# Output products of an attention layer, from columns on the partitions to tokens on the partitions

## The chip, the cores and the metric

The kernel runs on one core of a Trainium2 chip. The metric is the device time of one execution in microseconds. Most executions of one kernel agree within 0.3%; the kernel before took 551.26 us in the median of the first three runs (551.1 to 551.76). The span that a trace gives, from the first to the last instruction, is about 1.8 us shorter than the time of the same run (552.08 and 550.3 us for the profiled run of the kernel before).

Engine names in the profile: PE is TensorE's matmuls and PEld its weight loads, DVE the vector engine, ACT the scalar engine, POOL the one that issues some of the DMAs, SP the one that issues most of them and has no computation in these traces. STT in the prediction is DVE's operation SCALAR_TENSOR_TENSOR.

## The reference, cut to what matters

Attention with 16 query heads of 256, 512 keys, 2048 tokens; its output is multiplied by wo, gated, and added to x.

```python
# x: 2048 x 448;  o: 2048 tokens x 4096 (16 heads x 256);  wo: 4096 x 448
p = softmax(scores)                    # per head
o = einsum("bhqk,bhkd->bhqd", p, v)    # "P V"
s = o.transpose(...).reshape(B, Sq, Hq * Dh) @ wo
g = silu(ffn(xn))                      # the gate
return x + s * g
```

The kernel works on 512 tokens at a time. After the 16 heads of such a chunk it multiplies o by wo in one block, which this text calls a **burst**. There are four; each of the first three stands between a P V and Q matmuls of the next chunk, and the last one ends the kernel.

A burst uses Winograd's form of Strassen's scheme: tokens, contraction and columns are each halved, and seven products of sums take the place of eight. The sums of o are made by DVE (tile `sr`), those of wo once beforehand (tile `wt`).

## The kernel before: the parts that matter

wo's part is the stationary operand and o moves, so a product comes out with columns of the result on partitions. Each half has N2 = 192 columns, which are 128 + 64, so they are cut into pieces of 64 that fill the array two at a time; 64 columns are left over and multiplied plainly.

```python
N2 = (D - R) // 2                         # 192;  D = 448, R = 64, HC = 256 tokens

def product(j, b, rhs, hs, first, reads):     # one of the seven
    for h in hs:                              # two 64-column pieces, side by side in the array
        pair(0, HC, wt[:, WAT[j], h, 0:R], rhs(h), wt[:, WAT[j], h, R:P], rhs(h), ...)
    for h in hs[::2]:                         # the third piece, of two heads
        pair(HC, QC, wt[:, WAT[j], h, M2], rhs(h), wt[:, WAT[j], h + 1, M2], rhs(h + 1), False)
...
def plain():                                  # the 64 columns left over: 64 matmuls a burst
...
def turned(k):                                # four DMA transposes a burst: columns -> tokens
    dma_t(sT[:, :, k, :], xs[k], ...)
```

The last burst takes 14 heads. Then come the last two P V, and the last two heads are multiplied by wo apart, into banks where the burst's result is turned by matmuls with the identity:

```python
burst(c)                                      # c = 3, 14 heads
pv(late.pop(0)); pv(late.pop(0))
for t4, b, c0, c1 in ends[:3]:
    turn(t4, b, c0, c1)                       # matmuls with ident
...
    wo_mm(t4, b, ...)                         # o of heads 14 and 15, times wo
    wo_fin(c, t4, b, c0, c1)                  # scale, gate, add x, send
```

The gate is made early, by `down`, 128 tokens at a time, and waits in DRAM. DVE writes a tile of it into a ring of four slots, and SP sends it:

```python
K.op("dve", ... out=g2w[:, t % 4, :] ...)
dma("sp", g2d[t], g2w[:, t % 4, :], (b_g2w[t % 4],), (b_g2d[t],))
```

A scheduler in the kernel puts a semaphore wait wherever an operation reads what another engine wrote, or writes what another still reads.

The softmax here doesn't subtract the row's maximum and nothing guards it: scores larger than these inputs give would overflow.

Of the kernel before, what the change touches and what calls it, by code (L numbers as in the profile page):

```python
# [6 lines left out]
ALU = mybir.AluOpType  # L7
# [161 lines left out]
def bass_recurrent_scan__sliding_block_cached__geglu_ffn__prompt_kernel(  # L169
# [31 lines left out]
    CUT = D - P  # L201
# [5 lines left out]
    N2 = (D - R) // 2  # L207
# [3 lines left out]
    with es:  # L211
# [57 lines left out]
        b_xr = [[K.buf(a + (i * D + lo) * 2, (hi - lo) * 2) for lo, hi in ((0, CUT), (CUT, D))] for i in range(NXR)]  # L269
        tmp, a, _ = place("tmp", [P, 2, QC], F32)  # L270
        b_tmp = [[K.buf(a + (i * QC + lo) * 4, (hi - lo) * 4) for lo, hi in ((0, CUT), (CUT, QC))] for i in range(2)]

        tmpb, _, _ = place("tmpb", [P, 2, 2 * QC], BF16, at=a)
# [3 lines left out]
        wt, a_wt, a_w3 = place("wt", [P, 7, Hq, N2], F16)  # L277
# [3 lines left out]
        w3, _, rw_end = place("w3", [P, NCO, R], F16)  # L281
        w3b, _, _ = place("w3b", [P, NCO, R], BF16, at=a_w3)
        b_w3 = [K.buf(a_w3 + i * NCO // NB * R * 2, NCO // NB * R * 2) for i in range(NB)]
        NL = 4
        wo, a, a2 = place("wo", [P, NL, D], BF16, at=rw + WAT[0] * Hq * N2 * 2)
        assert NL * D <= Hq * N2
        b_wo = K.buf(a, NL * D * 2)
# [40 lines left out]
        a_c = b_p32[-1].hi - 8 * HC * 4  # L328
        assert a_c + 4 * HC * 4 >= a_p + 4 * HB * HC * 2
        cc, _, _ = place("cc", [P, 4, 2, HC], F32, at=a_c)  # L330
        b_cc = [[K.buf(a_c + (i * 2 + j) * HC * 4, HC * 4) for j in range(2)] for i in range(4)]
        g2w, a_s, a2 = place("g2w", [P, 4, D], BF16, at=at)
        b_g2w = sbuf_bufs(a_s, D * 2, 4)
        b_gz = sbuf_bufs(a_s, D * 2, 2)
        b_xz = [K.buf(a_s + (2 * D + lo) * 2, (hi - lo) * 2) for lo, hi in ((0, CUT), (CUT, D))]
        sT, _, at = place("sT", [P, 4, 3, P], BF16, at=at)
        b_sT = [K.buf(a_s, 12 * P * 2) for k in range(3)]
        b_xs = [K.buf() for k in range(4)]
        sN, _, at = place("sN", [P, 2, P], BF16, at=at)
        b_sN = K.buf(at - 2 * P * 2, 2 * P * 2)  # L340
# [66 lines left out]
        act(tmp[:, 1, 0:1], epst[:, :], ACT.Sqrt, (b_epst,), (b_tmp[1][0],))  # L407
# [134 lines left out]
        def down(c, pairs):  # L542
            for t4 in range(4):
                t = c * 4 + t4
                b = bk(pairs, t4)
                mms([(bank[b][:, 0:D], actT[:, c % 2, f, t4 * P:(t4 + 1) * P], wd[:, f, :], f == 0, f == NF - 1)
                     for f in range(NF)], [b_wd] + b_actT[c % 2], (b_ps[b],))
                s = t % 2
                act(tmp[:, s, 0:D], bank[b][:, 0:D], ACT.Tanh, (b_ps[b],), b_tmp[s], scale=0.5)
                K.op("dve", lambda e, t=t, b=b, s=s: e.scalar_tensor_tensor(  # L550
                    out=g2w[:, t % 4, :], in0=tmp[:, s, 0:D], scalar=1.0, in1=bank[b][:, 0:D],
                    op0=ALU.add, op1=ALU.mult), b_tmp[s] + [b_ps[b]], (b_g2w[t % 4],))
                dma("sp", g2d[t], g2w[:, t % 4, :], (b_g2w[t % 4],), (b_g2d[t],))
# [47 lines left out]
        act(tmp[:, 1, 0:1], nhalf[:, :], ACT.Gelu_apprx_tanh, (b_nhalf,), (b_tmp[1][0],))  # L601
# [28 lines left out]
        M2 = slice(P, N2)  # L630
# [4 lines left out]
        def cast_wt(j, i):  # L635
            if j == 7:
                sl, o, x, b = slice(i * NCO // NB, (i + 1) * NCO // NB), w3, w3b, b_w3
            else:
                sl, o, x, b = slice(i * Hq // NB, (i + 1) * Hq // NB), wt[:, WAT[j]], wtb[:, WAT[j]], b_wt[j]
            act(o[:, sl, :], x[:, sl, :], ACT.Copy, b[i:i + 1], b[i:i + 1], scale=WS)  # L640
# [6 lines left out]
        CASTS = [(18, (j, i)) for j in (0, 4, 7) for i in range(NB)] + [(40, (j, i)) for j in (2, 1) for i in range(NB)]  # L647
# [10 lines left out]
        for n in range(4, NU, 2):  # L658
# [11 lines left out]
            if n == 14:  # L670
                load_wt(0, 0, 0)
                load_wt(4, 0, 1)
                dma("pool", w3b[:, :, :], A_wo.rearrange("(c p) d -> p c d", p=P)[:, :, D - R:D], (), b_w3)
# [10 lines left out]
            if n == 32:  # L684
# [6 lines left out]
                for t in range(NXR):  # L691
                    dma("pool", xr[:, t, :], x_view[:, t, :], (), b_xr[t])
# [46 lines left out]
        def pv(m):  # L739
            h = m % Hq  # L740
            g, x = h // 2, m % NPT
            for e in range(2):
# [5 lines left out]
                o, f = (oTh, WS) if m < NS - LAG else (oT, 1.0)  # L748
                if e == 0:
                    act(o[:, i, :], bank[b], ACT.Copy, (b_ps[b],), (b_oT[i],), scale=f)  # L750
                else:
                    K.op("dve", lambda v, i=i, b=b, o=o, f=f: v.tensor_scalar(  # L752
                        o[:, i, :], bank[b], f, None, op0=ALU.mult), (b_ps[b],), (b_oT[i],))

        def wo_mm(t4, b, c0=0, c1=D, lo=NCO - 4, hi=NCO):

            mms([(bank[b][:, c0:c1], oT[:, i, t4 * P:(t4 + 1) * P], wo[:, i - NCO + NL, c0:c1], False, i == NCO - 1)
                 for i in range(lo, hi)], b_oT[lo:hi] + [b_wo], (b_ps[b],))

        def turn(t4, b, c0=0, c1=D):  # L760

            tok = slice(t4 * P, (t4 + 1) * P)
            lst = [(0, 0, tok, slice(0, P)), (P, 2, tok, HALF[0]), (N2, 1, tok, slice(0, P)), (N2 + P, 2, tok, HALF[1]),
                   (2 * N2, 3, slice(t4 % 2 * P, t4 % 2 * P + P), HALF[t4 // 2])]
            lst = [x for x in lst if c0 <= x[0] < c1]
            mms([(bank[b][:, lo:lo + k.stop - k.start], xs[j][:, q], ident[:, k], i == 0, False)
                 for i, (lo, j, q, k) in enumerate(lst)], b_xs + [b_ident], (b_ps[b],))

        def wo_end(t, c0, c1, mult, bt, y):

            x, bx = (xr[:, t % NXR, :], b_xr[t % NXR]) if t < NT - 1 else (g2w[:, 2, :], b_xz)
            g, bg = (g2[:, t % NG2, :], b_g2[t % NG2]) if t < NT - 2 else (g2w[:, t % 2, :], b_gz[t % 2])
            bx = [bx[i] for i in range(2) if (c0 < CUT, c1 > CUT)[i]]
            mult(g, bg)
            if t + NG2 < NT - 2:
                load_g2(t + NG2)
            add("dve", x[:, c0:c1], y[:, c0:c1], x[:, c0:c1], bt + bx, bx)
            dma("sp" if t >= NT - 4 else "pool", out_view[:, t, c0:c1], x[:, c0:c1], bx, ())
            if t + NXR < NT - 1:
                dma("pool", xr[:, t % NXR, :], x_view[:, t + NXR, :], (), b_xr[t % NXR])  # L780
            if t == NT - 5:
                K.reuse(b_gz + b_xz)
                for i in range(2):
                    dma("pool", g2w[:, i, :], g2d[NT - 2 + i], (b_g2d[NT - 2 + i],), (b_gz[i],))
                dma("pool", g2w[:, 2, :], x_view[:, NT - 1, :], (), b_xz)
# [4 lines left out]
        def wo_fin(c, t4, b, c0=0, c1=D):  # L790
            t = c * 4 + t4
            s = t % 2
            bt = [b_tmp[s][i] for i in range(2) if (c0 < CUT, c1 > CUT)[i]]
            if t4:
                y = tmpb[:, s, 0:D] if c0 == 0 else tmpb[:, s, CUT:CUT + D]

            def mult(g, bg):
                if t4 == 0:
                    K.op("dve", lambda e: e.scalar_tensor_tensor(  # L799
                        out=tmp[:, s, c0:c1], in0=bank[b][:, c0:c1], scalar=0.5, in1=g[:, c0:c1],  # L800
                        op0=ALU.mult, op1=ALU.mult), (b_ps[b], bg), bt)
                    return
                act(y[:, c0:c1], bank[b][:, c0:c1], ACT.Copy, (b_ps[b],), bt, scale=0.5)
                add("dve", y[:, c0:c1], y[:, c0:c1], g[:, c0:c1], bt + [bg], bt, ALU.mult)
            wo_end(t, c0, c1, mult, bt, tmp[:, s, :] if t4 == 0 else y)

        o_view = oTh.rearrange("p (h e) (r q) -> p e r h q", e=2, r=2)
        HALF = (slice(0, R), slice(R, P))
        xs = [xnT[:, k, 0:QC] for k in range(4)]

        def product(j, b, rhs, hs, first, reads):

            lst = []

            def pair(lo, hi, l0, r0, l1, r1, st):
                for u, l, r in ((0, l0, r0), (1, l1, r1)):
                    lst.append((bank[b][HALF[u], lo:hi], l, r, st, False))
            for h in hs:
                pair(0, HC, wt[:, WAT[j], h, 0:R], rhs(h), wt[:, WAT[j], h, R:P], rhs(h), first and h == hs[0])
            for h in hs[::2]:  # L820
                pair(HC, QC, wt[:, WAT[j], h, M2], rhs(h), wt[:, WAT[j], h + 1, M2], rhs(h + 1), False)
# [219 lines left out]
```

## Time and profile before

| | kernel before |
|---|---|
| time, median | 551.26 us |
| span in the trace | 550.3 us |
| PE busy | 98% of the span, 91% of the chain that ended last |
| first burst, start to the Q matmuls | 21.96 us |
| last burst, start to the end of the span | 32.05 us |

A burst is found in PE's timeline by its operands, `oTh,wt` and `sr,wt`. Matmuls are pipelined, so the cost of a group is read from the start of one to the start of the next, not from its busy time. The lines are in the prediction below.

### The profile page before, as it was taken

To read this page: it belongs to the slowest core of one execution; us is meant where nothing else is said; L and a number is where in the kernel's file an instruction comes from. 1 tells how busy PE (TensorE), PEld (TensorE's weight loads), DVE (VectorE), ACT (ScalarE), POOL (GpSimd) and SP (SyncE) were. 2 spreads that over 40 slices of the span, in tenths; PEclk is the share of its full clock that TensorE was granted. 3 is DMA by queue.
4 is the path that set the end of the run, shared out by engine and by line. 5 is a ranking of instruction groups with operands and counts; after the bars stand their busy time and mean duration, and the time that the engine had idled before them with its cause. 6 is when DMAs were issued, how large, how long until landed. Compare 5 with 4: busy or idle time off the path is not lost.

```text
span 550.3 us, 11945 instructions
## 1 busy us (share of the span) xinstructions
PE 540.5 (98%) x4649; PEld 294.7 (54%) x4674; DVE 360.0 (65%) x833; ACT 314.2 (57%) x795; POOL 41.4 (8%) x80
## 2 busy tenths in 40 slices
PE   8999999999999999999999999999999999999996
PEld 5554444445444444984444469544444974444594
DVE  6664735764457757945766786477568856767784
ACT  5433535763548858226866850498488037867603
POOL 1140500000000000003001000110100003002000
PEclk9999999999999999999999999999999999999999
DMA  9566289903325827313962850377267214855801
GB/s 286 125 184 151 61 280 307 162 1 84 92 48 115 154 58 153 65 31 76 169 139 59 151 123 7 57 155 154 74 112 158 45 31 113 155 116 135 149 33 35
DMA packets 177001, 63.29 MB, mean 115 GB/s; under 512 B 159808, under 2 KB 173648, under 8 KB 176944
## 3 DMA queue, kind: packets, MB, share of 16 engines
q1 hardware_dynamic: 172960, 52.76, 45.3%
q0 software_dynamic: 3216, 9.18, 5.8%
q8 instruction: 37, 0.61, 0.5%
q10 hardware_dynamic: 768, 0.57, 0.3%
q14 instruction: 20, 0.16, 0.1%
HBM read 20.22 MB, written 3.67 MB: 43 GB/s over the span
## 4 chain that ended last, share of the span: by engine, by line
PE 91%; DMA 2%; DVE 2%; ACT 2%; issue 1%; SPq 0%; ACTq 0%; DVEq 0%
PE bank L373 91%; ACT p L726 2%; DMA pT<-pn 2%; DVE pn L733 1%; DMA x<-in_A_x_dram 1%; DVE rden L730 0%; DVE tmpb L367 0%; SPq L358 0%; DVE qT L711 0%; DVE stats L420 0%; DVE tmp L799 0%; DVE sr L367 0%; DVE oTh L752 0%; ACT qT L364 0%; DVE g2w L367 0%
## 5 line engine op out<-in xcount | busy, mean ns | idle before, releaser
L726 ACT ACTIVATE p<-bank 128x512 f32<-128x512 f32 x256 | 150.5, 595 | 24.7 <-DVE pn L733 18.9
L373 PE MATMUL bank<-pT,va 128*128 128x512 bf16 x512 | 120.8, 379 | 0.3 <-DMA pT<-pn 0.3
L373 PE MATMUL bank<-kT,qT 128*128 128x512 bf16 x487 | 117.8, 379 | 2.3 <-ACT qT L364 1.0
L733 DVE TENSOR_SCALAR pn<-p,rden 128x512 bf16<-128x512 f32 x256 | 113.1, 484 | 9.6 <-DMA pT<-pn 5.5
L373 PE MATMUL bank<-xnT,wq 64*128 64x512 bf16 x768 | 94.9, 376 | 0.0
L373 PE MATMUL bank<-xnT,wgu 64*128 64x512 bf16 (+2 forms) x768 | 83.9, 350 | 0.5 <-ACT xnT L364 0.4
L373 PEld LDWEIGHTS bank<-pT,va 128*128 128x128 bf16 x512 | 49.6, 98 | 61.6 <-DMA pT<-pn 2.5
L373 PEld LDWEIGHTS bank<-kT,qT 128*128 128x128 bf16 x512 | 49.3, 98 | 62.0 <-issue 3.8
L364 ACT ACTIVATE qT<-bank 128x512 bf16<-128x512 f32 x76 | 44.1, 596 | 53.4 <-PE bank L373 51.8
L711 DVE CAST qT<-bank 128x512 bf16<-128x512 f32 x52 | 35.1, 692 | 44.0 <-PE bank L373 43.9
L373 PEld LDWEIGHTS bank<-xnT,wq 64*128 64x128 bf16 x768 | 36.7, 94 | 46.3 <-ACT p L726 2.1
L373 PEld LDWEIGHTS bank<-xnT,wgu 64*128 64x128 bf16 x768 | 37.1, 94 | 37.3 <-issue 0.7
L539 DVE TENSOR_TENSOR actT<-bank,gl 128x512 bf16<-128x512 f32 x56 | 37.8, 690 | 26.5 <-PE bank L373 19.9
L364 ACT ACTIVATE gl<-bank 128x512 bf16<-128x512 f32 x56 | 33.2, 597 | 37.1 <-PE bank L373 35.0
L730 DVE RECIPROCAL rden<-rsum 128x2 f32<-128x2 f32 x128 | 21.2, 166 | 48.5 <-ACT p L726 48.2
L726 ACT ACTIVATION_READ_ACCUMULATOR p<-bank 128x1 f32 x256 | 51.4, 201 | 0.0
L373 PE MATMUL bank<-wd,actT 128*128 128x448 bf16 x224 | 43.0, 353 | 0.0
L752 DVE TENSOR_SCALAR oTh<-bank 128x512 f16<-128x512 f32 x62 | 42.4, 684 | 0.0
L373 PE MATMUL bank<-sr,wt 128*64 128x256 f16 x744 | 41.5, 273 | 0.5 <-DVE sr L367 0.5
L364 ACT ACTIVATE xnT<-bank 128x256 bf16<-128x256 f32 (+2 forms) x12 | 4.9, 417 | 63.4 <-PE bank L373 62.8
L373 PEld LDWEIGHTS bank<-sr,wt 128*64 128x64 f16 x744 | 40.1, 110 | 1.4 <-DVE sr L367 0.7
L358 POOL DMA_DIRECT2D g<-g_all x14 | 7.5, 537 | 387.1 <-DVE tmpb L367 387.1
(71 smaller groups left out, 428.3 us busy)
## 6 DMA issues: line engine op xcount, KB each, us to landing
wtb<-in_A_wo_dram POOLq DMA_DIRECT2D x4, 768.0 KB, 7.2
wq<-in_A_wq_dram SPq DMA_DIRECT2D x2, 1536.0 KB, 9.2
va<-in_A_v_cache_dram SPq DMA_DIRECT2D x8, 256.0 KB, 6.4
pT<-pn SPq DMA_TRANSPOSE x128, 2.8
g_all<-g2w SPq DMA_DIRECT2D x16, 112.0 KB, 2.0
xr<-in_A_x_dram POOLq DMA_DIRECT2D x15, 112.0 KB, 2.3
wd<-in_B_w_down_dram SPq DMA_DIRECT2D x1, 1568.0 KB, 7.5
g<-g_all POOLq DMA_DIRECT2D x14, 112.0 KB, 2.3
```

The source lines that it names most:

```text
L358: K.op(q, lambda e, o=o, i=i: e.dma_start(o, i), reads, writes, dma=True)
L364: K.op("act", lambda e, o=o, i=i: e.activation(o, i, func, scale=scale), reads, writes)
L373: ins = e.matmul(o, lhsT=l, rhs=r, start=st, stop=sp, skip_group_check=True)
L539: K.op("dve", lambda e: e.tensor_tensor(actT[:, c % 2, f, :], bank[b + 1], gl[:, s, :], ALU.mult), (b_ps[b + 1], b_gl[s]), (b_actT[c % 2][ ...
L711: K.op("dve", lambda v, s=s, b=b: v.tensor_copy(qT[:, s, 1, :], bank[b + 1]), (b_ps[b + 1],), (b_qT[s][1],))
L726: K.op("act", lambda e, b=b, r=r, z=z: e.activation(p32[:, z, :], bank[b], ACT.Exp, scale=att_scale, accum_out=rsum[:, r:r + 1]), (b_ps[b] ...
L730: K.op("dve", lambda e, r=r: e.reciprocal(rden[:, r - 1:r + 1], rsum[:, r - 1:r + 1]), b_rsum[r - 1:r + 1], b_rden[r - 1:r + 1])
L733: K.op("dve", lambda e, r=r - 1 + t, z=(n - 1 + t) % NP32, y=y, t=t: e.tensor_scalar(pn[:, y, t, :], p32[:, z, :], rden[:, r:r + 1], None, ...
L752: K.op("dve", lambda v, i=i, b=b, o=o, f=f: v.tensor_scalar(o[:, i, :], bank[b], f, None, op0=ALU.mult), (b_ps[b],), (b_oT[i],))
```

## The change

Its intent: let o and its sums be stationary and wo's columns move. The product then has tokens on the partitions, as x, the gate and the output have them, so nothing is turned; 448 columns are two halves of 224 with nothing left over; and each matmul fills the whole array. The last burst takes all 16 heads, with the last two P V after its first 14 heads.

```diff
-    N2 = (D - R) // 2
+    N2 = D // 2                                   # 224
...
+            def product(j, b, lhs, hs, first, reads, ts=(0, 1)):
+                mms([(bank[b][:, t * N2:(t + 1) * N2], lhs(h)[:, t * P:(t + 1) * P], wt[:, WAT[j], h, :],
+                      first and h == hs[0] and t == ts[0], False) for h in hs for t in ts], ...)
...                                                # plain, turned, turn, wo_mm, wo_fin, the copies and folds of part: gone
+            first_two(0, allh[:Hq - LAG], True)   # heads 0 to 13
+            if last:
+                pv(late.pop(0))
+                pv(late.pop(0))
+            first_two(0, allh[Hq - LAG:], False)  # heads 14 and 15
...
-        g2w, a_s, a2 = place("g2w", [P, 4, D], BF16, at=at)
+        g2w, _, _ = place("g2w", [P, NXR, D], BF16, at=a)      # NXR = 3, in the place of xr
...
-                    out=g2w[:, t % 4, :], ...
+                    out=g2w[:, t % NXR, :], ...
```

wt grows with N2: each of the four loads of wo that feed it goes from 768 to 896 KB. To make room, the gate's ring shares the place of `xr` and has three slots.

## The prediction

> **What bounds the kernel now.** I read the busy table and the chain of waits first, then the groups by shape, then the timeline of TensorE (PE) around each block of output products (a "burst", one for each 512 tokens, four in all), then the timeline of the last 32 us.
>
> ```profile
> PE 540.5 (98%) x4649; PEld 294.7 (54%) x4674; DVE 360.0 (65%) x833; ACT 314.2 (57%) x795; POOL 41.4 (8%) x80
> ...
> PE 91%; DMA 2%; DVE 2%; ACT 2%; issue 1%; SPq 0%; ACTq 0%; DVEq 0%
> ```
>
> PE is busy 98% of the span and carries 91% of the chain that ended last; the granted clock is full throughout. So the three middle bursts are worth what they take of PE, and nothing else: the turning transposes, copies and folds that the change removes there are on engines with spare time (DVE 65%, ACT 57%). The first of those bursts, on PE's timeline:
>
> ```profile
> 220.13 1.89 PE L373 MATMUL bank<-pT,va 128*128 128x512 bf16 x8
> 221.95 2.81 PE L373 MATMUL bank<-oTh,wt 128*64 128x256 f16 x48
> 224.59 3.66 PE L373 MATMUL bank<-oTh,w 128*64 128x256 f16 x64
> 228.09 10.65 PE L373 MATMUL bank<-sr,wt 128*64 128x256 f16 x192
> 238.57 5.41 PE L373 MATMUL bank<-oTh,wt 128*64 128x256 f16 x96
> 243.91 0.82 PE L373 MATMUL bank<-xnT,wq 64*128 64x512 bf16 x6
> ```
>
> The reader is to see that no gap is marked, and that starts, not busy times, give the cost: 192 matmuls from 228.09 to 238.57 are 54.6 ns each, 109.2 ns for a pair that runs side by side in the two column halves of the array. The other two middle bursts start at 323.95 and 425.89 and last the same 21.95 us.
>
> The end is different: there PE really stops.
>
> ```profile
> 518.25 2.48 PE L373 MATMUL bank<-oTh,wt 128*64 128x256 f16 x42
> ...
> 521.20 9.57 PE L373 MATMUL bank<-sr,wt 128*64 128x256 f16 x168 [0.47 <-DVE sr L367]
> ...
> 541.88 0.65 PEld L373 LDWEIGHTS bank<-ident,xnT 128*128 128x128 bf16 x15 [0.41 <-DVE xnT L367]
> 541.89 0.77 PE L373 MATMUL bank<-ident,xnT 128*128 128x128 bf16 x15
> ...
> 542.49 2.44 PE L373 MATMUL bank<-wo,oT 128*128 128x448 bf16 x12
> ...
> 547.53 0.23 DVE L367 TENSOR_TENSOR g2w<-tmpb,g2w 128x128 bf16<-128x128 bf16 x1
> ```
>
> From the last burst's start to the end of the span is 550.3 - 518.25 = 32.05 us: products, a wait for the sums, the last two P V, 20 turning matmuls, 20 matmuls with wo for two heads, and a tail of ACT, DVE and output.
>
> **What the Trainium skill says.** "TensorE: Matmul & The Clock Gate", Back-to-back issue gap: N/2.4 + 2.5 ns per matmul of N columns when warm. The trace agrees: 109.2 ns a pair at N = 256 (formula 109.2), and eight P V matmuls of 512 start 1.73 us before the next eight, 216 ns each (formula 215.8). The same section also warns that in a stream with a weight load ahead of every matmul N = 128 takes some 81 ns, so short matmuls can be bound by the load. That is the danger here. The same page, Weight-path perf modes, says a full 128-column non-FP32 weight gets a fast load; "TensorEngine Tiling (Array Packing)", Restrictions, says column tiling disables it. The change leaves column tiling for full 128-column weights. The kernel before has a direct test of such loads: the 15 turning matmuls above, each with its own 128-column load. They stream 3 x (128+64+128+64+64) = 1344 columns and the wo matmuls start 0.60 us later; the formula gives 1344/2.4 + 15 x 2.5 = 598 ns. So a 128-column load (98 ns as listed) is repeated every 40 ns with no delay to the matmuls; the listed duration is latency, not spacing. That is bf16; the new loads are f16, which no run has shown yet.
>
> **The change, part by part.**
>
> Middle bursts, PE. Before: 7 products x 48 + 64 "plain" matmuls = 400, that is 200 pairs x 109.2 = 21.84 us; with two short gaps where the array's tiling changes (221.86 to 221.95, and about 0.1 at the end) 22.05 us from the last P V to the first Q matmul. After: N2 grows from 192 to 224 columns, the plain leftover goes, and each product is 16 heads x 2 token halves: 7 x 32 = 224 matmuls at 224/2.4 + 2.5 = 95.8 ns = 21.47 us, with one tiling change left: 21.57. That saves 0.48 us a burst, 1.4 us for three. It is little because the multiplications are almost the same: 7 x 32 x 224 = 50176 columns against 200 x 256 = 51200 streamed, 2% fewer.
>
> Middle bursts, other engines: out go four turning DMA transposes, four copies from one partition half to the other, four folds, and in each tile's closing step four DVE operations (1.24 us together in the timeline) become two of 0.39. All hidden, so 0. Do new waits appear? The sums: DVE starts them at 223.37, one group of four per 2.65 us; PE reaches the first group 64 matmuls = 6.1 us after the start, as before, and then uses one group per 3.07 us. No wait. The banks: six STT of 448 columns, about 0.62 us each (g2w row: 622 ns), must be done before Q's matmuls come; the last needs only the products before the final 3.07 us one, so they end about 1.5 us before it. No wait.
>
> Last burst, PE. Before, 14 heads and then the wo part for two heads; now all 16. New sum: first product's 14 heads, 28 x 95.8 = 2.68; two P V, 16 x 216 = 3.45; its last two heads 0.38; four groups of sums 128 x 95.8 = 12.27; two more products 6.13; in all 24.92 us. Put from the same start, 518.25, it ends at 543.2. The first product and the P V cover the wait for the sums: DVE's first sum is at 520.46, its first two at about 521.9, and PE now asks for them at 524.8. What may wait is P V for its transposes: the last is issued at 520.0 and lands after the median 2.7 us, at 522.7; the second P V starts at 520.93 + 1.73 = 522.66. I allow 0.1 us.
>
> Last burst, tail. DVE has, after the third product of the last group, 5 STT x 0.62, eight half-width multiplications or additions at about 0.27 (between 219 ns for 128 columns and 317 for 320), one more STT, and four more half-width ones: some 7 us, against 6.13 us of PE after that group, but it starts 2.2 us earlier as its banks fill, so it is done about 542.7, before PE. Behind PE's last matmul then stand its drain 0.2, one ACT copy of 224 columns 0.36 (between 272 and 437 ns rows), two DVE steps 0.55 with starts, and the output: before, from the end of the last DVE step (547.76) to the span's end was 2.54 us; I take 2.55. End: 543.3 + 0.2 + 0.4 + 0.6 + 2.55 = 547.0. Against 550.3 that saves 3.3 us.
>
> Elsewhere: weight casts and sums grow from 768 to 896 elements, four casts of w3 go; ACT and DVE wait for PE there, so 0. The gate's write ring has three slots for four: a tile comes every 2.65 us and its store lands in 2.1 us median, 6.5 at worst, less than three tiles. 0.
>
> Sum: 1.4 + 3.3 = 4.7 us; 551.26 - 4.7 = 546.5.
>
> **Rivals.** (1) Weight loads become the bound: 128 f16 columns every 224-column matmul at the listed 98 ns would make a burst 22.0 us: middle saving 0, last burst 0.5 worse, time about 548.5. For it: the skill's warning on short matmuls. Against: 40 ns loads in the turning. Without the fast load (128/1.2 = 107 ns by the page's formula, an estimate) each burst costs 24 us: about 556. (2) The tail becomes DVE-bound: if half-width steps took full-width time (0.39) and the STT 0.69, DVE would end about 2.5 us later, past PE's end, and time would be 548 to 549. Speaking against: the 219/317 ns rows. (3) The P V in the last burst wait for late transposes: one issue there took 2.3 us instead of 1.23 and landed after 4.6; a second such would put up to 2 us on PE: 548. (4) The removed transposes and copies had been slowing the middle in a way not seen: nothing in PE's gaps speaks for it, at most some tenths.
>
> **Range and chances.** Centre 546.5; (2) and (3) add up to 2 us, (1) about 2; below it, only a shorter tail or smaller gaps, about 1 us. Range 545.2 to 548.7. Faster by over 2% means under 540.2, and would need 11 us; PE's work alone forbids it. Slower by over 2% means over 562.3, and would need loads far slower than shown.
>
> **What would show it.** Right: starts of the burst matmuls 95.8 ns apart, 21.5 to 21.6 us from the last P V to Q in the middle; no marked PE gap in the last burst beyond a few tenths; the span from its start to the end near 28.8 us against 32.05; span about 545.6. Wrong: spacing of 98 ns or more, PE waiting for DVE at the banks of Q, a DVE step other than the last two ending after PE, or a P V that waits for pT.

## The result, and the profile after

547.8 us in the median (547.68 to 548.87, 4 runs) against 551.43 (551.1 to 551.76, 4 runs); the ratio is 0.9938, 95% interval 0.9921 to 0.9956. The span went from 550.3 to 545.9 us.

The first burst on PE's timeline after the change (columns: start, us busy, engine, line, operation, output <- operands, shapes, count, and in brackets idle time before it and what ended it):

```profile
221.18 1.89 PE L357 MATMUL bank<-pT,va 128*128 128x512 bf16 x8
222.91 6.30 PE L357 MATMUL bank<-wt,oTh 128*128 128x224 f16 x64
229.04 12.43 PE L357 MATMUL bank<-wt,sr 128*128 128x224 f16 x128
241.31 3.23 PE L357 MATMUL bank<-wt,oTh 128*128 128x224 f16 x32
244.47 0.82 PE L357 MATMUL bank<-xnT,wq 64*128 64x512 bf16 x6
```

128 matmuls from 229.04 to 241.31 are 95.9 ns each. From 222.91 to 244.47 are 21.56 us, where it was 21.96, and the short gap before the burst is gone: eight P V matmuls take 1.73 us, and 221.18 + 1.73 is 222.91. The burst also starts 0.96 us later than before.

The end of the last burst, all engines:

```profile
517.56 2.86 PE L357 MATMUL bank<-wt,oTh 128*128 128x224 f16 x28 [0.33 <-ACT oTh L348]
...
520.25 3.62 PE L357 MATMUL bank<-pT,va 128*128 128x512 bf16 x16
...
524.09 12.43 PE L357 MATMUL bank<-wt,sr 128*128 128x224 f16 x128
...
536.36 6.30 PE L357 MATMUL bank<-wt,oTh 128*128 128x224 f16 x64
...
541.55 0.28 DVE L351 TENSOR_TENSOR xnT<-xnT,g 128x224 bf16<-128x224 bf16 x1 [0.18 <-ACT xnT L348]
...
542.69 0.36 ACT L348 ACTIVATE xnT<-bank 128x224 bf16<-128x224 f32 x1 [1.18 <-PE bank L357]
543.08 0.28 DVE L351 TENSOR_TENSOR xnT<-xnT,g 128x224 bf16<-128x224 bf16 x1 [0.95 <-ACT xnT L348]
543.39 0.27 DVE L351 TENSOR_TENSOR xr<-xnT,xr 128x224 bf16<-128x224 bf16 x1
```

The reader is to see PE without a marked gap from 517.56 on, and DVE waiting at 541.55 and at 543.08 for ACT's copy of what PE has just finished: DVE is not the bound of the tail.

Where the 4.4 us of span come from, by the bursts' starts. The run with four ring slots (below) is put beside them.

| stretch, us | before | after | difference | after, four slots |
|---|---|---|---|---|
| start to the first burst | 221.95 | 222.91 | +0.96 | 221.42 |
| first to second burst | 102.00 | 101.32 | -0.68 | 101.32 |
| second to third | 101.94 | 101.45 | -0.49 | 101.33 |
| third to last | 92.36 | 91.88 | -0.48 | 91.88 |
| last burst to the end | 32.05 | 28.34 | -3.71 | 28.35 |
| span | 550.3 | 545.9 | -4.4 | 544.3 |

These are single profiles, and the kernel before is not quite steady. Two other runs with the same code in the last stretch had 31.46 and 31.84 us there, without the wait of 0.47 us for the sums, so the gain of that stretch is 3.1 to 3.7 us. Its start varies too: this profile has two waits in its first 9 us (0.62 and 0.36 us), and the three variants of the kernel before that were run below reach the first burst at 221.52 to 221.82. That is part of why the spans differ by 4.4 us and the times by 3.6.

So the middle and the end gave about what was expected or more, and one thing before the first burst took 0.96 us back. The list of waits names it (total us, times, longest):

```profile
PE bank L357 <- DVE g2w L534: 1.2, 1, 1.2
```

PE waits 1.2 us, once, for DVE's write of a gate tile into the ring. In DVE's timeline of the kernel before, the four gate tiles of that place come at the pace of their matmuls:

```profile
67.73 0.62 DVE L550 SCALAR_TENSOR_TENSOR g2w<-tmp,bank 128x448 bf16<-128x448 f32 x1 [1.47 <-PE bank L373]
70.38 0.62 DVE L550 SCALAR_TENSOR_TENSOR g2w<-tmp,bank 128x448 bf16<-128x448 f32 x1 [2.03 <-ACT tmp L364]
73.09 0.62 DVE L550 SCALAR_TENSOR_TENSOR g2w<-tmp,bank 128x448 bf16<-128x448 f32 x1 [2.09 <-ACT tmp L364]
75.74 0.62 DVE L550 SCALAR_TENSOR_TENSOR g2w<-tmp,bank 128x448 bf16<-128x448 f32 x1 [2.03 <-ACT tmp L364]
```

After the change, the fourth of them and what follows:

```profile
79.20 0.62 DVE L534 SCALAR_TENSOR_TENSOR g2w<-tmp,bank 128x448 bf16<-128x448 f32 x1 [5.84 <-DMA g_all<-g2w]
...
79.88 0.82 PE L357 MATMUL bank<-xnT,wgu 64*128 64x512 bf16 x6 [1.23 <-DVE g2w L534]
```

The tile needs the slot of the tile three before it, whose store was issued at 68.03 and landed at 79.08, 11 us later. PE then waits for the bank that this tile leaves.

### The profile page after: what moved, and what is told of

Read it like the earlier page. It is cut to its first block, busy times and chain, and to the rows that moved or that the text cites. A ratio compares the mean times of both kernels' runs of the same rounds, so it can differ in the third digit from the quotient of the medians.

```text
span 545.9 us, 10453 instructions
## 1 busy us (share of the span) xinstructions
PE 537.6 (98%) x3955; PEld 294.5 (54%) x3980; DVE 350.0 (64%) x785; ACT 305.1 (56%) x770; POOL 38.6 (7%) x78
## 4 chain that ended last, share of the span: by engine, by line
PE 93%; DMA 2%; ACT 2%; DVE 2%; issue 1%; DVEq 0%; ACTq 0%
PE bank L357 92%; DMA g_all<-g2w 2%; ACT p L703 1%; PE bank L474 1%; DVE pn L710 1%; ACT qT L348 0%; DVE rden L707 0%; DVE g2w L534 0%; PE bank L455 0%; DVE qT L688 0%; ACT oTh L348 0%; ACT xnT L348 0%; DVE xnT L351 0%; DVE xr L351 0%; DVE gl L387 0%
## 5 line engine op out<-in xcount | busy, mean ns | idle before, releaser
L357 PE MATMUL bank<-wt,sr 128*128 128x224 f16 x512 | 49.7, 259 | 0.0
L357 PEld LDWEIGHTS bank<-wt,sr 128*128 128x128 f16 x512 | 49.1, 98 | 0.0
L348 ACT ACTIVATE xnT<-bank 128x224 bf16<-128x224 f32 (+2 forms) x12 | 4.4, 400 | 71.7 <-PE bank L357 70.9
L348 ACT ACTIVATE oTh<-bank 128x512 f16<-128x512 f32 x66 | 38.9, 590 | 4.6 <-PE bank L357 4.6
```

The source lines that it names most:

```text
L348: K.op("act", lambda e, o=o, i=i: e.activation(o, i, func, scale=scale), reads, writes)
L357: ins = e.matmul(o, lhsT=l, rhs=r, start=st, stop=sp, skip_group_check=True)
```

## The experiments

The theory after the result: (a) a 224-column matmul with its own 128-column load costs 95.8 ns, with room to spare; (b) the last burst gains both by what it no longer does and by its order; (c) three ring slots, together with larger loads of wo that slow the stores, cost PE its 1.2 us; (d) the turning was worth next to nothing. Each had a rival. Nine kernels ran.

### A fourth ring slot

The fourth slot lies in the first `g2` tile, which is idle at that time.

```diff
-                    out=g2w[:, t % NXR, :], ...
+                    out=gslot(t), ...             # four slots: g2w[0..2] and g2[0]
-                    K.reuse([b for y in b_xr for b in y])
+                    K.reuse([b for y in b_xr for b in y] + b_g2)
```

> The changed kernel with a fourth slot in the gate's write ring (the slot lies in the first g2 tile, which is idle until the attention part). Theory: the three-slot ring made one gate tile wait 5.84 us for the store of three tiles before, and TensorE lost 1.2 us by it near 79 us; with four slots the wait of g2w for its own store is 0, the first burst starts about 1.1 us earlier than 222.91, and the span is 544.7 us instead of 545.9. Rival: the stores land up to 11 us late, so a fourth slot only moves the wait to another tile, or TensorE loses the time to another wait: span 545.6 or more.

Measured: 546.27 us against 551.39, ratio 0.9907 (0.9891 to 0.9924); span 544.3. The wait of g2w for its store is gone from the list of waits, PE's with it, and the first burst starts at 221.42. The wait cost 1.5 us by the start of the first burst and by the span (545.9 to 544.3 is 1.6), a little more than the 1.2 us that PE's wait showed. By PE's starts, from the first of the gate's matmuls of that place to the first Q matmul are 51.40 us after the change (63.89 to 115.29) and 50.00 in this run; so 1.40 us are the wait's, and the other 0.1 lies before it. The theory holds; the wait moved nowhere else, as the table's other stretches show.

### Three ring slots in the kernel before

```diff
-                    out=g2w[:, t % 4, :], ...
+                    out=g2w[:, t % 3, :], ...     # and in the store
```

> The kernel before with three slots in the gate's write ring, nothing else. Theory (it takes the larger wo loads of the changed kernel, 896 for 768 KB, and three slots together): stores land in at most about 6.5 us as before, TensorE has no wait of 1 us near 79 us, span 550.3 within 0.3. Rival (three slots alone do it): g2w waits some us for its store and TensorE loses about 1.2 us, span 551.5.

Measured in one look: 551.14 us, span 549.3; no wait of g2w for its store, none of PE for g2w. So three slots alone do not make the wait. Something in the changed kernel makes the stores later.

### The loads of wo held back

Two of the four wo loads are issued by POOL just before those gate tiles. This run makes them wait for the last of the tiles, with the ring left at three.

```diff
-                load_wt(2, 1, 1)
-                load_wt(1, 1, 0)
+                load_wt(2, 1, 1, b_g2d[7:8])      # read-after-write on the store of gate tile 7
+                load_wt(1, 1, 0, b_g2d[7:8])
```

> The changed kernel with its three ring slots, but the two 896 KB loads of wo held until the gate of tile 7 is stored. Theory (the stores of the gate land late because they share the DMA engines with these loads; ring and loads together make the wait): g2w no longer waits 5 us for its store, TensorE's 1.2 us wait near 79 us is gone, span 544.5 within 0.3. Rival (the stores are late whatever the loads do): the wait stays, span 545.9; or the later loads are missed by the casts and TensorE waits there.

Measured in one look: 547.12 us, span 545.3. The view of the DMAs between 62 and 82 us, of the changed kernel:

```profile
wtb<-in_A_wo_dram POOLq DMA_DIRECT2D x2, 896.0 KB, 10.4
...
g_all<-g2w SPq DMA_DIRECT2D x4, 112.0 KB, 7.7
```

and of this run:

```profile
wtb<-in_A_wo_dram POOLq DMA_DIRECT2D x2, 896.0 KB, 11.3
g_all<-g2w SPq DMA_DIRECT2D x4, 112.0 KB, 1.6
```

The last number is the median time from issue to landing. With the loads out of the way a store takes 1.6 us instead of 7.7, and the 5.84 us wait at 79 us is gone. So this much is shown: the stores are late because of the loads of wo beside them, and three slots do not cover that. In the changed kernel the second load landed at 78.75 and the three stores that were waiting at 79.08, 79.55 and 79.83. The edit also moves two 112 KB loads of POOL that stand behind those of wo, but they are not the cause: in the four-slot run they come later as well, and the stores there still took up to 10.7 us.

The span fell by 0.6 us and not by the theory's 1.4. From the gate's matmuls to the first Q matmul it is 49.99 us, so this wait is gone in full. But at the ring's first use, near 50 us, the other two loads do the same: there g2w waited 4.72 us (3.18 in the changed kernel), PE has a marked wait of 0.20 us, and by its starts that stretch was 0.38 us longer.

What stays open is why these loads crowd the stores more than those of the kernel before did. There the view between 60 and 82 us says:

```profile
wtb<-in_A_wo_dram POOLq DMA_DIRECT2D x2, 768.0 KB, 7.1
...
g_all<-g2w SPq DMA_DIRECT2D x4, 112.0 KB, 3.9
```

A sixth more bytes took 10.4 us instead of 7.1, and the slowest store 11.0 instead of 6.4, although the kernel before had three 112 KB loads of x at that place besides. So size alone, as theory (c) has it, does not account for it. The rows that are loaded have another length (448 bytes for 384) and another start; no run separates these.

### The last two P V ahead of the first product

```diff
+            if last:
+                pv(late.pop(0)); pv(late.pop(0))
             first_two(0, allh[:Hq - LAG], True)
-            if last:
-                pv(late.pop(0))
-                pv(late.pop(0))
```

> The changed kernel with the last two P V put ahead of the first product in the last burst, all else as it is. Theory (the order is worth much): P V of the last head must wait for its transpose, which lands about 522, so TensorE starts it 3.1 us later than it could, and the 28 products that had filled this time come after: span 548.6 us, 2.7 us more. Rival (the gain of the last burst is all from the turning, the wo matmuls and the old tail being gone): span within 0.4 us of 545.9.

Measured: 549.92 us, ratio 0.9971 (0.9956 to 0.9986); the changed kernel's is 0.9938 (0.9921 to 0.9956), so this is slower by 0.33%, 1.8 us. PE's timeline:

```profile
516.17 1.89 PE L357 MATMUL bank<-pT,va 128*128 128x512 bf16 x8
518.38 1.89 PE L357 MATMUL bank<-pT,va 128*128 128x512 bf16 x8 [0.32 <-ACT oTh L348]
521.81 1.89 PE L357 MATMUL bank<-pT,va 128*128 128x512 bf16 x8 [1.54 <-DMA pT<-pn]
523.53 3.23 PE L357 MATMUL bank<-wt,oTh 128*128 128x224 f16 x32
```

The last P V starts 1.7 us later than PE could, as its transpose has not landed. To compare the ends, take the end of head 13's P V (its start and 1.73 us) to the end of the span: 32.15 us in the kernel before, 30.50 here, 28.83 after the change. So of 3.3 us, about 1.65 come from what the last burst no longer does (turning by matmuls, separate wo matmuls, the old tail) and 1.67 from putting the first product's 14 heads where PE would wait. The first figure is less sure than the second: with the two other profiles of the same old code (31.55 and 31.93 us) it would be 1.05 and 1.43. The theory's 2.7 us was too high, since the transpose landed 3.8 us after head 13's P V and not 4.8 as in the changed kernel.

### 13 heads instead of 14

The changed kernel's first line of the last burst shows a wait of 0.33 us for ACT's `oTh`. Head 13 is among the 14, and its P V has just ended.

```diff
-            first_two(0, allh[:Hq - LAG], True)
+            H1 = Hq - LAG - last
+            first_two(0, allh[:H1], True)
```

> The run with four ring slots (span 544.3), and the first piece of the last burst's first product takes 13 heads instead of 14. Head 13 is the one whose P V has just ended, so TensorE waits for its copy by ACT (0.32 us marked, 0.48 us from the end of that P V to the product). Theory: this wait goes, and the transpose of head 15 lands soon enough: span 543.85. Rival (the P V of head 15 is bound by its transpose's landing, so what is won at the start is lost there, and more since two heads less fill the time): a TensorE wait for pT appears, span 544.3 or more.

Measured (with four ring slots): 546.46 us, ratio 0.9897 (0.9881 to 0.9913); span 544.9. Both theory and rival are partly right:

```profile
514.46 1.89 PE L360 MATMUL bank<-pT,va 128*128 128x512 bf16 x8
516.19 2.65 PE L360 MATMUL bank<-wt,oTh 128*128 128x224 f16 x26
518.68 1.89 PE L360 MATMUL bank<-pT,va 128*128 128x512 bf16 x8
520.76 1.89 PE L360 MATMUL bank<-pT,va 128*128 128x512 bf16 x8 [0.20 <-issue]
```

The wait at the start is gone (514.46 + 1.73 = 516.19), and most of it is back before the last P V, which starts 2.08 us after the one before it instead of 1.73. The profile marks this gap "issue", but the last transpose landed at 520.67, 0.09 us before that P V. From the end of head 13's P V to the end of the span are 28.71 us, against 28.83 with 14 heads.

### Two sum products between the last two P V

```diff
             if last:
                 pv(late.pop(0))
+                of_sums(0, FOUR[:2])              # 16 matmuls of the first group of sums
                 pv(late.pop(0))
```

> As the 13-head run, and two of the four sum products of the first group moved between the last two P V, to give the last transpose 1.5 us more. If the transposes are in time anyway: span as the 13-head run, 543.85 within 0.2. If they bind there: this one is faster than the 13-head run, by up to its wait for pT, and reaches 543.85.

Measured, with 13 heads and four slots: 545.93 us (545.72 to 546.22), ratio 0.9886 (0.9870 to 0.9903); span 544.4. The last P V starts without a wait, and the same stretch is 28.31 us, 0.52 less than with 14 heads and 0.40 less than with 13 alone. By the trace the wait for the last transpose did bind the run before. That the moved products cured it is not shown: in this profile the last transpose landed at 520.11, before 520.30, where that P V would have stood without them. By the times, three versions of 0.9907, 0.9897 and 0.9886 are not told apart, as their intervals overlap. Against the changed kernel's 0.9938 (0.9921 to 0.9956) this version is faster, and so it beats both the kernel before and the change, though by less than 2%.

### Smaller pieces

The products' matmuls are cut into two of 112 columns in the first burst and four of 56 in the second, each with its own weight load; the result is the same.

```diff
+                np_ = {0: 2, 1: 4}.get(c, 1)
+                w = N2 // np_
-                mms([(bank[b][:, t * N2:(t + 1) * N2], lhs(h)..., wt[:, WAT[j], h, :], ...)
+                mms([(bank[b][:, t * N2 + k * w:t * N2 + (k + 1) * w], lhs(h)..., wt[:, WAT[j], h, k * w:(k + 1) * w], ...)
```

> The changed kernel with every 224-column product matmul cut into two of 112 columns in the first burst and four of 56 in the second, each with its own weight load; the third burst is left. It measures what a 128-column f16 load costs. Theory (loads are hidden at 224 columns with room): matmuls 49.2 ns apart in the first burst, so 22.1 us from its start to the Q matmuls against 21.56; in the second, where a matmul streams only 25.8 ns, the load shows: about 40 ns apart as in the turning of the kernel before, 36 us. Rival (the load is just hidden at 224, and its 98 ns are its spacing, or 53 ns): 448 x 98 = 44 us, or 448 x 53 = 23.9 us, in the first burst.

Measured in one look: 550.43 us, span 548.6. The first burst took 22.12 us, as theory (a) had it. The second, on PE's timeline:

```profile
331.06 13.67 PE L357 MATMUL bank<-wt,sr 128*128 128x56 f16 x512
344.57 0.29 PE L357 MATMUL bank<-wt,oTh 128*128 128x56 f16 x5
```

512 matmuls from 331.06 to 344.57 are 26.4 ns each, not 40. The whole burst took 23.95 us (324.44 to 348.39) and not 36. Even there the load hardly shows. So a 128-column f16 load fits into 26 ns, and at 224 columns it has more than three times what it needs. One reserve: the four pieces of a product load the same 128 columns four times in a row, so for loads that differ each time the runs show only the 40 ns of the turning. The 40 ns of the prediction were only the pace of that example, where the matmuls themselves took 40.

### The turning twice, and not at all

Two runs on the kernel before. One sends each turning transpose of a middle burst twice; the other sends them after the first burst only, so that the second and third use stale data. That result is wrong, though the comparison with the reference still passed, presumably since what is added to x is too small for it to tell.

```diff
-                    dma_t(sT[:, :, k, :], xs[k], ...)
+                    [dma_t(sT[:, :, k, :], xs[k], ...) for _ in range(2)]     # first run; sN likewise
```
```diff
-                if not last:
+                if c == 0:                                                    # second run
```

> The kernel before with each of the four turning DMA transposes of a middle burst sent twice (12 more transposes in all, same result). Theory (the turning is hidden, so its removal is worth nothing): span 550.3 and time within 0.2% of the kernel before. Rival (the turning slows the middle by its DMA traffic, or by the closing steps that wait for it, and its removal is part of the gain): time up by 0.5 us or more for the double, with TensorE waits after the bursts.

> The kernel before with the four turning transposes sent after the first burst only; the second and third reuse what the first left, so their results are wrong on purpose. The doubled transposes cost 5 us by delaying the transposes of P, so it is open what one dose costs. Theory (one dose is almost hidden): from the second to the third burst's start 101.9 us as before (101.94), from the third to the fourth 92.0 against 92.36, where the profile of before marks a TensorE wait of 0.30 us for pT; in all 0.4 us less. Rival (the turning costs TensorE more than its marked waits): each of these stretches 0.5 us or more shorter than before.

Doubled: 557.38 us against 552.08, ratio 1.0094 (1.0061 to 1.0127), 5 us more. The list of waits of that run:

```profile
DVE tmpb L367 <- DMA sT<-xnT: 9.4, 3, 3.3
...
PE bank L373 <- DMA pT<-pn: 4.8, 3, 2.8
```

DVE waits for the turned tiles, and later PE waits 4.8 us in three places for the transposes of P, which come through the same SP queue. Yet one of those transposes took 6.5 us to land when the extra ones had been done for 7.5 us before its issue, and why is not settled by these runs. The theory fell as it stood: the turning was hidden, but a second dose was not. What one dose cost is the other run's to say: 551.42 us against 551.52, ratio 0.9996 (0.9979 to 1.0013). The stretch from the second to the third burst was 102.11 us, and from the third to the last 91.93, against 101.94 and 92.36. So taking the turning away is worth nothing that the times show, and at most some tenths in one stretch. The copies and folds on ACT and DVE, which the change removes as well, stayed in this run; they were not tested by themselves.

## Why the prediction was right

The measured 547.8 us lies in the range of 545.2 to 548.7, 1.3 us above its centre. The mechanisms that it named for PE were right; that the range held is in part luck, since its upper 2 us were meant for rivals 2 and 3, which did not come, and most of that was used up by a wait that it had ruled out. Point by point:

- **The bound.** PE, and so only PE's path counts: right. The removal of transposes was worth nothing by itself, as it said. (One reading there is wrong and without consequence: the four closing operations on DVE take some 1.1 us together by their group means, 281 + 218 + 184 + 392 ns; the 1.24 us are those of three folds.)
- **Middle bursts, PE.** 95.8 ns a matmul and 21.57 us were predicted, 95.9 ns and 21.56 us measured, with no new wait. The three stretches gave 1.65 us for a predicted 1.4, although the third already bears the new wait for head 13 (next point but one), some 0.4 us more than the old gap there; and the kernel before had a wait of 0.30 us for a transpose in that stretch. These tenths are not told from run-to-run changes.
- **Rival 1, weight loads.** It fell, and by more than the prediction thought (26.4 ns).
- **Last burst, PE.** 24.92 us were predicted from its start. The last group of 64 matmuls starts 18.80 us after the burst (536.36 - 517.56) and 64 x 95.8 ns are 6.13: 24.93. Missed was that the first piece asks for head 13, whose copy was just being made. The prediction had the P V wait only for their transposes, with 0.1 us allowed; the trace has 0.33 us of marked wait, 0.49 us from the end of that P V. It did not hurt much, since the transpose would have taken back most of it. Rival 3, a late transpose, came close: the last one landed at 521.90, and its P V could start at 521.98.
- **Tail.** 3.7 us were predicted from PE's last matmul to the end, 3.4 measured: from DVE's last step (543.66) to the end are 2.24 us, where the kernel before had 2.54. Rival 2, a DVE-bound tail, fell: DVE waited 0.95 us before its last pair. (The 542.7 for DVE's earlier steps does not follow from the prediction's own figures: 7.0 us from 2.2 us before 537.1 end at about 541.9. In the trace they ended at 541.37, 23.8 us after the burst's start, so 0.6 us sooner than said.)
- **The gate's ring.** This is the step that failed: "a tile comes every 2.65 us and its store lands in 2.1 us median, 6.5 at worst, less than three tiles. 0." It was worth 1.4 to 1.5 us. The landing time was read from the kernel before, while the change itself altered the loads that crowd those stores; it became 11.0 us, more than three tiles' 8. The three-slot run of the kernel before shows that the reading was right for the kernel that it came from.

The sum was 4.7 us; by the spans it came to 4.4, with 0.96 us lost before the first burst, and 0.25 and 0.4 us more than expected in the middle and in the last stretch (no more than the single profiles differ by). With the ring mended the kernel took 546.27 us, close to the predicted 546.5, though smaller errors cancel in that: the tail was shorter than expected, and the wait for head 13 was not foreseen.

## What to carry to other kernels

Here the matmuls already streamed at their pace, and another layout of the same multiplications was worth only the columns and gaps that it saved, 0.4 us a burst; the larger gain lay where the engine stopped, in the last burst, and half of it or more came from filling the wait for a late transfer with work that does not depend on it. When a change takes a slot from a ring, check the landing time of its transfers with the traffic that the new kernel will have beside them, not with the old. And doubling a hidden cost does not say what its removal is worth (here 5 us against none that the times show); for that it must be taken away.

## What the Trainium skill lacked or had wrong

- "TensorE: Matmul & The Clock Gate", Back-to-back issue gap: it gives about 81 ns a matmul at N = 128 and 131 at N = 512 for streams with a load ahead of each, and says that N/2.4 + 2.5 ns undercounts there for small N. Here such streams follow the formula: 26.4 ns at 56 columns (25.8 by formula), 95.9 at 224 (95.8), 216 at 512 (215.8).
- The same page, LDWEIGHTS (loading the stationary operand): P/1.2 is 107 ns for 128 columns; its section Weight-path perf modes says that the fast weight load has measured some 2x, and gives 4x as theory for fp8. The load's record lasts 98 ns, but loads of 128 f16 columns followed each other every 26.4 ns, four times as fast as the formula (the same columns four times in a row; 15 different bf16 loads of the turning came every 40 ns).
- "TensorEngine Tiling (Array Packing)", Key Properties: it says that a change of tiling mode drains TensorE, without a figure. At the start of each middle burst of the kernel before, from full to half-width tiles, about 0.09 us lay between the P V and the products; without the change of mode there was none (221.18 + 1.73 = 222.91). That the drain is the reason was not tested.
- "DMA: Bandwidth & Descriptors", Issuing engines are not separate DMA queues, says that transfers of all issuers interleave, but not by how much a small one is delayed: a 112 KB store took 1.6 us without the loads of wo and up to 11 us beside two 896 KB loads of another issuer's queue, and it landed only after the second of them (79.08 after 78.75).
